# Attention with a beacon prefix, then a gated feed-forward: one key quarter turned earlier, and the last weight third and the output weights issued later

## The chip, the cores and the metric

The kernel runs on one core of a Trainium2 chip. The metric is the device time of one execution in microseconds. Four executions of the kernel before are given, and one more was profiled.

## The reference

Eight batches of eight heads go through causal attention, each with 16 extra "beacon" keys that every query sees. The result is laid out as a matrix of 4608 tokens by 512 features and goes through a feed-forward layer with a gate.

```python
def _attn_ref(q, k, v, beacon_k, beacon_v):        # q, k, v: (8, 8, 576, 64)
    k_all = np.concatenate([beacon_k, k], axis=2)  # 16 + 576 keys
    v_all = np.concatenate([beacon_v, v], axis=2)
    scores = scale * np.matmul(q, k_all.transpose(0, 1, 3, 2))
...
    scores = np.where(causal, -1000000000.0, scores)
...
    return np.matmul(a, v_all)                     # a: softmax of scores

def _moe_ref(x, w_gate, w_val, w_out):             # x: (4608, 512), d_ff 1536
    gate = np.maximum(x @ w_gate, 0.0)
    val = x @ w_val
    return (gate * val @ w_out)
```

## The kernel before

The whole order of work is written out by hand: every engine runs its own instructions in the order in which the program names them, and waits only where a datum or a buffer is missing.

**Attention.** A batch has 592 key rows (16 beacon rows and 576), cut into five key tiles of 128 rows, the last one short. Its queries are cut into chunks of 240, 256 and 80. A unit of work is one group of four heads, one chunk and one key tile: TensorE makes the scores (line 368), ScalarE the exponentials (line 376), and GpSimd clears what lies above the diagonal (the affine selects of line 384). Two units make a step, seven steps a batch. When the units of a chunk are done, TensorE multiplies the exponentials by the values and by ones (line 418), and VectorE divides (lines 430 to 443). So the first product with the values of a batch waits for the values, for the exponentials and for GpSimd's selects.

**Feed-forward.** A tile is 512 tokens. Twelve "up" groups make it (the gate in line 464, the values in line 473, both four matmuls of 512 columns, then lines 467 and 475), and four "down" groups of twelve matmuls each (line 483) use all twelve slices of `wo`. Up group number nf reads columns 128·nf to 128·nf+127 of `wg` and `wv`. The groups fill TensorE between the attention steps: the plan has seven steps for batch 0, four steps without attention (7 to 10, with 0, 3, 3 and 2 groups), seven steps for batch 1 with one group each (11 to 17), two steps without attention with four groups each (18 and 19), and then batches 2 to 7. `s2` is 11, the first step of batch 1; batch 2 begins with step 20 and batch 3 with step 27.

**Queries and keys must lie transposed.** There are three ways. In batch 0 a quarter (256 rows, four heads) is loaded by SyncE (line 281), cast by VectorE or ScalarE (line 285), turned by eight TensorE transposes (line 300) and copied out of PSUM by VectorE or ScalarE (line 301). In batch 1 GpSimd issues loads that cast on the way (line 289), and TensorE turns them in `turn_two`. From batch 2 on SyncE loads rows (line 244), GpSimd casts them (lines 263 and 259), and SyncE issues transposing DMAs (line 268).

**Weights.** The first 256 columns come by SyncE and are cast (lines 339, 345). All others are loaded by GpSimd with a cast on the way: `load_w` issues one DMA for each of two groups (line 330), `load_wo` one DMA for six slices (line 348).

**The queues.** SyncE issues its DMAs in program order, and so does GpSimd; GpSimd's DMA issues stand in one line with its selects and casts. Eight DMAs of a queue have semaphores of their own: in the compiled order the ninth waits until the first has landed. The lists `after(step, ...)` (later half of a step), `between` (after the first unit's scores), `mid` (after the first unit's exponentials) and `behind` fix where an action stands. The values of batch 1 are loaded by SyncE behind a one-element memset on GpSimd (line 241, `held`), which stands on GpSimd's queue behind the eight loads of batch 1's queries and keys.

In step 0 of batch 0 the order is: scores of the first unit, `turn_next`, exponentials of the first unit, `turn_third`, scores of the second unit, `turn_first("q", 1, 0)`. A quarter is named by its half of the rows and its half of the heads: ("k", 0, 1) is keys, first half of the rows, second four heads.

Of the kernel before, what the change touches and what calls it, by code (L numbers as in the profile page):

```python
# [159 lines left out]
def kernel(  # L160
# [38 lines left out]
    wg = const.tile([P, KM, d_ff], BF16, name="wg")  # L199
    wv = const.tile([P, KM, d_ff], BF16, name="wv")  # L200
# [127 lines left out]
    def load_w(dst, src, n0, n1, groups=(0, 1)):  # L328
        for g in groups:
            nc.gpsimd.dma_start(  # L330
                dst[:, 2 * g:2 * g + 2, n0:n1],
                src[2 * g * P:2 * (g + 1) * P, n0:n1].rearrange("(p a) n -> p a n", a=2))
# [14 lines left out]
    def load_wo(i0, i1):  # L347
        nc.gpsimd.dma_start(wo[:, i0:i1],
                            moe_w_out.rearrange("(ko ki) n -> ki ko n", ki=P)[:, i0:i1])
# [177 lines left out]
    with tc.manual_schedule():  # L527
        batches = {}
        dve, act, pool = nc.vector.tensor_copy, nc.scalar.copy, nc.gpsimd.tensor_copy
# [8 lines left out]
        def load_tails(x):  # L538
            x.tails = [x.load_rows(k[x.b, :, 512:]), x.load_rows(q[x.b, :, 512:])]
# [10 lines left out]
        first = batches[0] = Batch(0)  # L550
# [18 lines left out]
        def turn_first(n, i, g, move):  # L569
            ps = f_ps.tile([P, 2, 2, P], BF16, name="f")  # L570
            return first.turn_quarter(n, i, g, ps, move)
# [6 lines left out]
        warm_up(2, 256)  # L578
        first.cast_quarter("k", 0, 1, dve)
        first.cast_quarter("q", 0, 1, act)  # L580

        def turn_two(x, i, k_bank):
            ps = {"k": k_bank.tile([P, NP, 2, P], BF16, name="f" if k_bank is f_ps else "s"),
                  "q": f_ps.tile([P, NP, 2, P], BF16, name="f")}
            for move in [x.turn_quarter(n, i, g, ps[n][:, 2 * g:2 * g + 2],
                                        dve if n == "k" else act)
                         for g in range(2) for n in "kq"]:
                move()
# [12 lines left out]
        def after(step, action):  # L601
            later_half.setdefault(step, []).append(action)

        second = batches[1] = Batch(1)
        s2 = BASE[1]
# [1 line left out]
        held = []  # L607

        def turn_next():
            turn_first("k", 0, 1, dve)()  # L610
            first.cast_quarter("k", 1, 0, dve)
            held.append(turn_first("q", 0, 1, act))
            first.cast_quarter("q", 1, 0, dve)

        def turn_third():
            held.pop()()
            turn_first("k", 1, 0, dve)()

        between[0], mid[0] = turn_next, turn_third
        behind[0] = lambda: turn_first("q", 1, 0, dve)()  # L620
        after(0, lambda: first.cast("v", 0, pool))
# [27 lines left out]
        after(6, lambda: [cast_w(wv, raw_v, 256, g, act) for g in range(2)])  # L649
        second.beacon = second.load_rows(beacon_k[1])  # L650
        load_tails(second)
        for n0 in (768, 1152):
            after(6, lambda n0=n0: load_w(wg, moe_w_gate, n0, n0 + 384))
            after(6, lambda n0=n0: load_w(wv, moe_w_val, n0, n0 + 384))

        def load_second(i):
            for g in range(2):
# [6 lines left out]
            after(7, lambda t=t: second.load("v", t, t == 0))  # L664
        for t in range(NKT):
            after(s2 - 1 + t // 2, lambda t=t: second.cast("v", t, pool))
        after(s2 - 2, lambda: load_wo(0, 6))
        after(s2 - 1, lambda: load_wo(6, 12))

        def cast_small(x):  # L670
            x.beacon = x.cast_rows(x.beacon, dve)
# [186 lines left out]
```

## Time and profile before

| | us |
|---|---|
| median of four executions | 394.16 (392.57 to 394.45) |
| profiled execution: its time | 393.09 |
| profiled execution: its span | 391.4 |

| engine | busy us | share of the span |
|---|---|---|
| TensorE, matmuls (PE) | 375.2 | 96% |
| VectorE (DVE) | 205.4 | 52% |
| ScalarE (ACT) | 192.9 | 49% |
| GpSimd (POOL) | 127.6 | 33% |

The page cuts the span into 40 slices of 9.8 us; a digit is the busy share in tenths. Its chain of work that ended last is 88% TensorE and 6% DMA. The mean granted TensorE clock is 0.991 of full speed. Both DMA queues use the same 16 engines: the queue of SyncE (q1, 139,024 packets, 44.48 MB) and that of GpSimd (q0, 9,056 packets, 5.24 MB as written in bf16). All DMA shares count the time of packets in flight, so a share over 100% means that packets overlap. In a timeline each row has its start, its length, the engine (SPq is SyncE's queue), the line, the operation, what it writes and reads, and in brackets the idle time before it with the instruction that ended it.

### The profile page before, as it was taken

Reading aid. Unit: us, or ns where it says so; the run is one execution under the profiler, and the core shown is the slowest. Engines: PE = TensorE matmul, PEld = TensorE weight load, DVE = VectorE, ACT = ScalarE, POOL = GpSimd, SP = SyncE. Lnnn points to the kernel's source line nnn. Section 1 sums busy time; section 2 is a strip of 40 time slices with the busy share of each in tenths; the row PEclk is TensorE's granted clock in tenths of the full one; section 3 lists DMA queues with packets and bytes.
Section 4 is the critical chain, followed back from the end, with each engine's and each line's share of the span. In section 5 each row is a group of like instructions: output and inputs, shape, how many; then the busy total and the mean of one; then the engine's idle time right before and its main releaser. Section 6 shows DMA issues by size and latency. Waiting matters only on the chain.

```text
span 391.4 us, 10271 instructions
## 1 busy us (share of the span) xinstructions
PE 375.2 (96%) x4297; PEld 188.2 (48%) x4297; DVE 205.4 (52%) x342; ACT 192.9 (49%) x270; POOL 127.6 (33%) x220
## 2 busy tenths in 40 slices
PE   6889859999999999999999999999999999999995
PEld 2554425544555455445454545444545454444443
DVE  4868336653665655476537563666465645512320
ACT  4773436435655655465546554656366633323321
POOL 1697275423553444143514350535020200000000
PEclk9999979999999999999999999999999999999999
DMA  8999999777995997399439943996300011002002
GB/s 215 233 177 185 192 179 222 150 173 171 194 146 162 186 210 123 107 205 177 98 110 190 201 87 105 198 173 120 97 28 2 2 65 46 0 32 77 0 28 86
DMA packets 148132, 50.44 MB, mean 129 GB/s; under 512 B 133616, under 2 KB 143600, under 8 KB 148080
## 3 DMA queue, kind: packets, MB, share of 16 engines
q1 hardware_dynamic: 139024, 44.48, 56.1%
q0 software_dynamic: 9056, 5.24, 9.7%
q8 instruction: 35, 0.57, 0.7%
q14 instruction: 17, 0.14, 0.2%
HBM read 38.34 MB, written 9.44 MB: 122 GB/s over the span
## 4 chain that ended last, share of the span: by engine, by line
PE 88%; DMA 6%; POOL 2%; ACT 2%; issue 1%; SPq 0%; DVE 0%; POOLq 0%
PE f L483 24%; PE f L464 23%; PE s L473 12%; PE f L473 10%; PE s L368 8%; PE ab L418 7%; PE os L418 3%; DMA raw<-in_v_dram 3%; DMA wg<-in_moe_w_gate_dram 2%; ACT e L376 1%; DMA wide<-in_q_dram 1%; PE f L300 1%; PE f L418 1%; POOL wv L330 1%; POOL hwide L289 0%
## 5 line engine op out<-in xcount | busy, mean ns | idle before, releaser
L376 ACT ACTIVATE e<-s 128x1024 bf16<-128x1024 f32 (+2 forms) x112 | 104.8, 963 | 29.0 <-PE s L368 28.9
L464 PE MATMUL f<-xT,wg 128*128 128x512 bf16 x432 | 112.2, 382 | 0.3 <-DMA hwide<-in_k_dram 0.3
L467 ACT ACTIVATE g<-f 128x512 f32<-128x512 f32 x108 | 64.5, 597 | 82.3 <-PE f L464 80.3
L483 PE MATMUL f<-wo,hT 128*128 128x512 bf16 (+1 forms) x444 | 96.7, 374 | 0.0
L384 POOL TENSOR_SCALAR_AFFINE_SELECT e<-e 128x512 bf16<-128x512 bf16 (+2 forms) x80 | 47.0, 599 | 149.9 <-ACT e L376 144.8
L430 DVE RECIPROCAL r<-os 128x80 f32<-128x80 f32 (+2 forms) x43 | 57.6, 1339 | 58.0 <-PE os L418 58.0
L475 DVE TENSOR_TENSOR hT<-g,s 128x512 bf16<-128x512 f32 x60 | 41.2, 687 | 66.3 <-PE s L473 65.2
L473 PEld LDWEIGHTS <-wv 128*128 128x128 bf16 x432 | 42.4, 98 | 52.7 <-issue 3.1
L483 PEld LDWEIGHTS <-hT 128*128 128x128 bf16 x444 | 41.9, 98 | 47.4
L464 PEld LDWEIGHTS <-wg 128*128 128x128 bf16 x432 | 39.6, 98 | 46.8 <-issue 1.3
L473 PE MATMUL s<-xT,wv 128*128 128x512 bf16 x240 | 61.6, 379 | 0.0
L486 ACT COPY ob<-f 128x512 f32<-128x512 f32 (+1 forms) x37 | 21.3, 575 | 73.9 <-PE f L483 71.9
L475 DVE TENSOR_TENSOR hT<-g,f 128x512 bf16<-128x512 f32 x48 | 33.0, 688 | 37.0 <-PE f L473 32.4
L473 PE MATMUL f<-xT,wv 128*128 128x512 bf16 x192 | 50.2, 384 | 0.2 <-ACT qT L301 0.2
L263 POOL CAST half<-raw 128x512 bf16<-128x512 f32 (+2 forms) x60 | 36.8, 625 | 23.0 <-DMA raw<-in_k_dram 8.7
L418 PE MATMUL ab<-e,v 128*32 128x80 bf16 (+4 forms) x1320 | 39.3, 234 | 4.5 <-POOL e L384 4.5
L368 PE MATMUL s<-qT,kT 64*128 64x80 bf16 (+3 forms) x704 | 36.1, 236 | 1.4 <-ACT e L376 0.9
L418 PEld LDWEIGHTS <-v 128*32 128x32 bf16 (+1 forms) x1408 | 26.5, 98 | 14.5 <-issue 7.2
L368 PEld LDWEIGHTS <-kT 64*128 64x128 bf16 x704 | 20.6, 97 | 25.9 <-issue 23.8
L418 PE MATMUL os<-e,ones 128*32 128x240 bf16 (+4 forms) x660 | 32.2, 233 | 0.0
L259 POOL CAST v<-raw 128x512 bf16<-128x512 f32 (+1 forms) x40 | 26.6, 668 | 15.5 <-DMA raw<-in_v_dram 15.0
L443 DVE TENSOR_TENSOR xT<-ab,r 128x480 bf16<-128x480 f32 (+2 forms) x45 | 24.9, 554 | 0.8
(66 smaller groups left out, 136.4 us busy)
## 6 DMA issues: line engine op xcount, KB each, us to landing
out_dram<-ob SPq DMA_DIRECT2D x35, 256.0 KB, 2.2
raw<-in_q_dram SPq DMA_DIRECT2D x25, 256.0 KB, 4.8
raw<-in_v_dram SPq DMA_DIRECT2D x24, 256.0 KB, 5.2
raw<-in_k_dram SPq DMA_DIRECT2D x19, 256.0 KB, 4.5
raw<-in_v_dram SPq DMA_DIRECT2D x8, 224.0 KB, 3.8
wo<-in_moe_w_out_dram POOLq DMA_DIRECT2D x2, 768.0 KB, 9.1
raw<-in_k_dram SPq DMA_DIRECT2D x6, 224.0 KB, 4.4
raw<-in_v_dram SPq DMA_DIRECT2D x8, 160.0 KB, 4.6
```

Of the source, the lines that this page charges most:

```text
L259: copy(self.v[:n, t].rearrange("p (h a d) -> p h a d", a=2, d=C), raw[:n].rearrange("p (h d a) -> p h a d", a=2, d=C))
L263: copy(h[:n], raw[:n])
L368: nc.tensor.matmul(self.s[:, a, c + j * n:c + (j + 1) * n], kT[rows, 2 * g + j, k0:k0 + P], qT[rows, 2 * g + j, q0:q0 + n], start=True, st ...
L376: nc.scalar.activation(e[:, :k * 4 * n].rearrange("p (k a x) -> p a k x", k=k, a=2), self.s[:, :, :k * 2 * n].rearrange("p a (k x) -> p a ...
L384: nc.gpsimd.affine_select(out=cols[:, :, :m], in_=cols[:, :, :m], pattern=[[0, 4], [1, m]], compare_op=ALU.is_ge, fill=0.0, base=base, cha ...
L418: nc.tensor.matmul(o[:, q0 - cq0:q0 - cq0 + n], w, e[:kr, 2 * (hh % 2) + hh // 2], start=(i == 0 and part != 1), stop=(i == self.last), sk ...
L430: nc.vector.reciprocal(self.r[:, :n], self.os[:, :n])
L464: nc.tensor.matmul(g[:, :n], wg[:, ki, nf * P:(nf + 1) * P], x[:, ki], start=(ki == 0), stop=(ki == KM - 1))
L467: nc.scalar.activation(gs[:, :n], g[:, :n], AF.Relu)
L473: nc.tensor.matmul(u[:, :n], wv[:, ki, nf * P:(nf + 1) * P], x[:, ki], start=(ki == 0), stop=(ki == KM - 1))
L475: nc.vector.tensor_mul(self.h[:, nf, c0:c1], gs[:, :n], u[:, :n])
L483: nc.tensor.matmul(o[:, n], self.h[:, nf, ms * P:(ms + 1) * P], wo[:, nf, n], start=(nf == 0), stop=(nf == NF - 1))
```

## The change

Three things are moved; nothing is added or removed.

- The second key quarter ("k", 0, 1) is turned before the first scores of batch 0, not after them. Its VectorE copy moves with it. The cast of the quarter ("q", 1, 0) moves on VectorE from before to behind the copy of ("k", 1, 0).
- The last third of `wg` and `wv` (columns 1152 to 1535, four DMAs) is issued on GpSimd's queue behind the eight loads of batch 1's queries and keys and the memset that holds batch 1's values, not ahead of them.
- The two halves of `wo` are each issued one step later: the first behind the casts of the first two value tiles of batch 1, the second behind those of the next two.

```diff
         first.cast_quarter("q", 0, 1, act)
+        turn_first("k", 0, 1, dve)()
...
         def turn_next():
-            turn_first("k", 0, 1, dve)()
             first.cast_quarter("k", 1, 0, dve)
             held.append(turn_first("q", 0, 1, act))
-            first.cast_quarter("q", 1, 0, dve)

         def turn_third():
             held.pop()()
             turn_first("k", 1, 0, dve)()
+            first.cast_quarter("q", 1, 0, dve)
...
-        for n0 in (768, 1152):
-            after(6, lambda n0=n0: load_w(wg, moe_w_gate, n0, n0 + 384))
-            after(6, lambda n0=n0: load_w(wv, moe_w_val, n0, n0 + 384))
+        after(6, lambda: load_w(wg, moe_w_gate, 768, 1152))
+        after(6, lambda: load_w(wv, moe_w_val, 768, 1152))
...
-        after(s2 - 2, lambda: load_wo(0, 6))
-        after(s2 - 1, lambda: load_wo(6, 12))
+        after(s2 - 2, lambda: load_w(wg, moe_w_gate, 1152, 1536))
+        after(s2 - 2, lambda: load_w(wv, moe_w_val, 1152, 1536))
+        after(s2 - 1, lambda: load_wo(0, 6))
+        after(s2, lambda: load_wo(6, 12))
```

In the compiled order the other differences follow from these: four issues (line 330) stand behind the memset of line 241 on GpSimd, each `wo` issue (line 348) stands one block further back, up group 9 on TensorE waits for the weights' four DMAs, and SyncE's order is the same in both kernels.

## The prediction

> **What bounds the kernel now.** I read the page's slices first, then who waited on TensorE, then the chain, then SyncE's queue. The slices:
>
> ```profile
> PE   6889859999999999999999999999999999999995
> PEclk9999979999999999999999999999999999999999
> DMA  8999999777995997399439943996300011002002
> ```
>
> TensorE is full from slice 6 (58.7 us) on. Its one hole behind the start is slice 5, where the clock drops as well. The DMA engines are full in the same stretch. The waits of TensorE up to 100 us name one long one, and the chain of that stretch tells where it comes from:
>
> ```profile
> PE ab L418 <- POOL e L384: 4.5, 1, 4.5
> ```
>
> ```profile
> 40.44 0.09 POOL raw L241
> ...
> 41.39 10.14 DMA raw<-in_v_dram
> 51.53 0.05 issue
> 51.58 0.62 POOL v L259
> 52.21 0.78 issue
> 52.99 0.60 POOL e L384
> 53.59 0.04 issue
> 53.63 0.59 PE ab L418 x6
> ```
>
> Batch 1's values are held until the memset at 40.44, land at 51.53, and GpSimd casts them, issues half of `wo` (0.78) and clears the exponentials before TensorE resumes at 53.63. TensorE had stopped at 49.11. The table by stages shows what follows:
>
> ```profile
> 53.63:60.50 6.87, 6.87 (x73) 2.98 (x73) 3.00 (x3) 2.48 (x3) 4.19 (x8) 0.56 1.05 168
> ```
>
> The granted clock is 0.56 for 6.87 us. This is what the change is near, and by this view alone it should pay. The view that decides is another one, SyncE's queue in order of time. From 40.55 to 123 us no row of it is more than 0.8 us behind the end of the one before: SyncE issues without a rest, first batch 1's values, then all of batches 2 and 3. The last transposed keys and queries that the first step of each needs are these:
>
> ```profile
> 86.48 1.24 SPq L268 DMA_TRANSPOSE kT<-half  x1
> 87.81 1.21 SPq L268 DMA_TRANSPOSE qT<-half  x1
> ...
> 118.67 1.22 SPq L268 DMA_TRANSPOSE qT<-half  x1
> ```
>
> By the DMA view of 87 to 90 and of 118 to 120 us a query transpose lands 2.4 us after its issue starts: 90.2 and 121.1. TensorE reaches batch 2's first scores at 92.82, so slack there is 2.8 us. At batch 3 it is none:
>
> ```profile
> 120.73 0.81 PE L368 MATMUL s<-qT,kT 64*128 64x240 bf16 x12
> ```
>
> Twelve such score matmuls take 0.60 at 44.68 and at 92.82. Here they take 0.81: the last four stand until about 121.2, when the queries have landed. So behind TensorE's own work lies a second path of almost the same length, SyncE's queue.
>
> **The change, part by part.**
>
> *The key quarter.* Eight transposes (0.64, the row at 10.33) go ahead of the first scores, which move from 7.75 to about 8.2; the first exponentials move from 8.37 to 8.8. The VectorE copy (0.69) starts at 8.25 and not 8.94, the next cast ends 0.7 earlier, the second scores start at 10.45 and not 10.90 (then ScalarE's query copy, behind the first exponentials, is last). But the cast of ("q", 1, 0) now stands behind a key copy: cast 10.95 to 11.45, turn to 12.1, copy to 12.9, against 12.81 before. The scores that waited for this copy (12.86) start at 12.95. Sum: +0.1. Bounds: −0.5 if the second scores' gain were carried on, +0.5 if the first scores' delay were.
>
> *The last weight third.* Four issues of 0.72 (2.86 us of GpSimd) leave the place ahead of batch 1's loads. These eight can be issued from 29.4 on, held by the rule that the ninth waits for the first: the fourth issue after it, 0.8 each, gives a memset at about 36.1 and not 40.44. SyncE's queue starts 4.3 us earlier. What it meets is the engines' work. From 28.6 to 53 us they are full; packets of the two queues show the rates:
>
> ```profile
> q0 software_dynamic: 465, 0.48, 93.1%
> q1 hardware_dynamic: 448, 0.11, 28.9%
> ```
>
> That is 45 to 48 us: 155 `wo` packets a us, and one value packet beside each. Alone, values run at 850 a us (3,398 in the 4 us from 49), batch 1's loads at 704 (3,519 in the 5 us from 38). Now the four weight DMAs lie beside the values: 1,024 packets of 768 bytes, some 200 a us with one value packet each, 39.4 to 44.4. The first two value tiles (2,048 packets) have 900 by then and the rest in 1.4 us; with 1.3 to land, they are there at 47.0, not 51.5. With the 2.1 us of cast, issue and select TensorE resumes at 49.1. It gets there at 48.1, since the stalls of `turn_two` on its loads (0.29 and 0.30) and the wait behind them go, 1.0 in all. So 53.63 becomes 49.1 (−4.5), a gap of 1.0 in place of 4.52, and the half clock is gone: the up group in it took 1.82 + 1.71, the next one at full clock (60.50) 0.97 + 0.86, so 1.7 there, and of the other 3.34, some of it at full clock, 1.2. Together −2.9. Bounds: 0 if values land as before, −8.4 if no gap is left.
>
> Its new deadline: group 9 needs the third at about 50.5 and it has landed by 46: no cost.
>
> *The output weights.* First half issued at about 47.7 and moving from 50, second at 51.5 and moving behind it, 768 packets at 155 a us each: landed at about 61.3. The first down group would read slice 6 at 66.52 − 7.4 + 1.35 = 60.5, so it waits 0.8; bounds 0 and 2.5. Each issue (0.82) lies on GpSimd ahead of selects and casts; the first one was on the path before as well, the second is hidden by the selects' waits for ScalarE. At the first down group TensorE is therefore 6.5 ahead.
>
> *Where this goes.* It does not reach the end, because SyncE's queue is not 6.5 us ahead. The bytes that have to move before batch 2's keys are the same, and the engines were full already. At 60 us, before: `wo` done at 59.4, SyncE's queue alone for 5 us (48.4 to 53.4). After: `wo` done at 60, SyncE's queue alone for 5 us (44.4 to 49.2, less 0.8 without packets). Between 53.4 and 55 the engines were nearly idle (58 GB/s, with 185 after it), so 1.1 us of work is lost before and 0.8 after. Shift of SyncE's queue: −0.3. Bounds: −4.3, its start's own shift, if packets shared the engines for free, and +1. Then batch 2's first step stands: TensorE is there at 93.07 − 6.5 = 86.6 and waits 3.4 for the queries at 90.0. It keeps 3.0. At batch 3 it is there at 118.2 and waits for 120.8: 2.6 more. From there on the order is as before.
>
> A rule speaks against the change here. Trainium skill, *DMA: Bandwidth & Descriptors*, section "Issuing engines are not separate DMA queues": transfers of all issuing engines interleave on the same 16 engines, and another queue saves only issue time. The row above shows one packet beside the other, at no loss for `wo`. Were the sharing free, as that row alone suggests, the sum would be −4.3; by the rule it is −0.3. I take the rule, for the full engines.
>
> Sum against the profiled execution: 393.09 + 0.1 − 0.4 = 392.8. The same step from the median of 394.16 is **393.9**. The 0.4 are SyncE's 0.3 and what is left of the wait at 121.
>
> **The rivals.** "Measurable" is 0.5% here, 2.0 us.
>
> *The queue does come forward.* SyncE starts 4.3 us earlier and keeps it, because value packets slip in beside the weights' unseen. For it: 448 packets slipped in at 45 to 48. Against: from 53 on the queue is short of engine time. Then batch 3's queries land at 116.8, and the time is 394.16 − 4.3 = 389.9. Chance 0.15, with smaller shifts over 2.0 in it.
>
> *Slower: the wait ahead of batch 3 stops the clock.* Before, the gap of 4.5 us was paid early and hidden by the slack up to 121. Now TensorE stands at batch 2 (3.4) and batch 3 (2.6). The row: a gap of 4.52 is followed by 6.87 us at 0.56. Trainium skill, *TensorE: Matmul & The Clock Gate*, Part 1: half rate after an idle window of about 3.4 us, full rate after a busy one, windows free-running. By the row alone 2.6 is far from 4.5 and costs 0; by the rule it is 0.8 short of the least gap that can hold a window. Behind batch 3 no slack is left, so it costs 3.4 in full: 393.9 + 3.4 = 397.3. It decides from a gap of 3.4 at batch 3. At batch 2 the same loss is harmless, as it fills the wait at batch 3. Chance 0.13; with SyncE's queue over 2 us late, 0.17 for slower.
>
> *The change does nothing at 49 us.* The third beside the values keeps them to 51.5. TensorE's gap stays, slack at batch 2 and 3 as before: 394.2. Chance 0.08.
>
> **How the numbers follow.** Forecast 0.60, nothing at 49 us 0.08: same 0.68. Faster 0.15. Slower 0.17. Its own range is 392.5 to 395.5 (queue −1.5 to +1.5). The range is 391.6 to 396.8: it leaves out a tenth at each end, most of the first rival and most of the second.
>
> **What would show it.** TensorE's wait at 53 us and the half clock are gone, values landed at 46 to 48, first down group at 59 to 62. Batch 2's query transpose is still issued at 87 to 88 and batch 3's at 118 to 119. The waits of TensorE name line 368 with a releaser on SyncE's queue or qT, 2 to 4 us each, at about 86 and 118. The hole in slice 5 moves to slices 8 and 12. I am wrong if these transposes come over 2 us earlier, if batch 2's scores start before 89, or if the clock drops at 120.

## The result, and the profile after

| | kernel before | changed kernel |
|---|---|---|
| median | 393.38 us (63 executions, 391.99 to 396.07) | 392.21 us (42 executions, 388.98 to 394.43) |
| profiled execution: its time | 393.09 us | 391.63 us |
| profiled execution: its span | 391.4 us | 389.9 us |

The ratio is 0.9965, with a 95% interval of 0.9954 to 0.9977: about 1.4 us faster (the two medians differ by 1.2), inside the 0.5% that the prediction called no change. The four executions whose median, 394.16, the prediction starts from are among the 63.

The slices of the page of the changed kernel, to be held against the three rows that the prediction shows first:

```profile
PE   7879979998999999999999999999999999999995
PEclk9999989999999999999999999999999999999999
DMA  8999999978995996499449943995300011002002
```

The hole in slice 5 has shrunk (7 where there was 5), and the clock there is 8 and not 7. There is a small new hole in slice 9 (88 to 97 us). TensorE's largest group of waits (their sum, their number, the longest), and the chain from 37.7 to 52 us:

```profile
PE ab L418 <- POOL e L384: 5.2, 4, 2.4
```

```profile
37.72 0.09 POOL raw L241
...
38.67 10.28 DMA raw<-in_v_dram
48.95 0.05 issue
49.00 0.62 POOL v L259
49.62 0.80 issue
50.42 0.60 POOL e L384
51.03 0.04 issue
51.07 0.59 PE ab L418 x8
```

It is the same chain as before, earlier by 2.6 us: the memset that releases the values starts at 37.72 and not 40.44, the values land at 48.95 and not 51.53, TensorE resumes at 51.07 and not 53.63, after a gap of 2.42 us and not 4.52. But that wait now has company: 5.2 us in four waits, where it was one of 4.5. The clock behind it, from the table by stages (start and end, length, then the busy time of each engine; the clock is the third number from the end):

```profile
51.07:54.50 3.43, 3.43 (x33) 1.46 (x33) 2.05 (x2) 1.03 (x2) 3.42 (x7) 0.57 1.11 171
```

Half the clock for 3.43 us, against 6.87 us before. The first down group starts at 62.41 (before 66.45 in the same view) and batch 2's first scores at 88.91 (before 92.82): TensorE is 3.9 us ahead. SyncE's queue is not. These are the issues of the last query transposes that the first steps of batches 2 and 3 need, shown for before at 87.81 and 118.67. Below, "the last query transpose" of a batch always means this one.

```profile
86.73 1.21 SPq L268 DMA_TRANSPOSE qT<-half  x1
88.00 0.57 SPq L244 DMA_DIRECT2D raw<-in_beacon_k_dram  x1
88.62 0.42 SPq L244 DMA_DIRECT2D raw<-in_k_dram  x1
```

```profile
117.39 1.21 SPq L268 DMA_TRANSPOSE qT<-half  x1
```

They are 1.1 and 1.3 us ahead. Where TensorE gives the difference back is seen on GpSimd from 92 us, and on TensorE at 95.77. First the same two casts of the kernel before, with no wait ahead of them, then the changed kernel:

```profile
94.81 1.17 POOL L263 CAST half<-raw 128x512 bf16<-128x512 f32 x2
```

```profile
92.48 0.61 POOL L263 CAST half<-raw 128x512 bf16<-128x512 f32 x1 [1.53 <-DMA raw<-in_k_dram]
93.65 0.62 POOL L263 CAST half<-raw 128x512 bf16<-128x512 f32 x1 [0.55 <-DMA raw<-in_q_dram]
94.49 0.64 POOL L259 CAST v<-raw 128x512 bf16<-128x512 f32 x1 [0.23 <-DMA raw<-in_v_dram]
95.08 1.81 POOL L384 TENSOR_SCALAR_AFFINE_SELECT e<-e 128x512 bf16<-128x512 bf16 x3
```

```profile
95.77 0.29 PE L418 MATMUL ab<-e,v 128*32 128x128 bf16 x8 [1.70 <-POOL e L384]
```

GpSimd's selects for batch 2 stand behind casts of batch 3's first tiles, and those casts wait for loads that SyncE issued at 88.62 and later, right behind batch 2's transposes. TensorE waits 1.70 us. The same happens at 112.21 (0.73). 3.9 − 1.7 − 0.7 leaves 1.5 us, and the two spans differ by 1.5. Batch 3's first scores come at 119.61 (before 120.73, where the last four of them waited about 0.2 more). Behind them the changed kernel is 1.3 us ahead, and it still is at 200.75 (before 202.04).

### The profile page after: what moved, and what is told of

Its sections match the earlier page's. It is cut to its first block, busy times and chain, and to the rows that moved or that the text cites. A ratio compares the mean times of both kernels' runs of the same rounds, so it can differ in the third digit from the quotient of the medians.

```text
span 389.9 us, 10272 instructions
## 1 busy us (share of the span) xinstructions
PE 374.0 (96%) x4297; PEld 187.2 (48%) x4297; DVE 204.4 (52%) x342; ACT 192.9 (49%) x270; POOL 128.2 (33%) x220
## 4 chain that ended last, share of the span: by engine, by line
PE 79%; DMA 10%; SPq 5%; POOL 3%; DVE 1%; issue 1%; ACT 0%; POOLq 0%; DVEq 0%
PE f L483 23%; PE f L464 21%; PE s L473 11%; PE f L473 9%; PE ab L418 6%; PE s L368 6%; DMA raw<-in_v_dram 6%; SPq L244 3%; PE os L418 2%; DMA wv<-in_moe_w_val_dram 2%; DMA raw<-in_k_dram 1%; SPq L281 1%; DMA raw<-in_q_dram 1%; POOL e L384 1%; SPq L268 1%
## 5 line engine op out<-in xcount | busy, mean ns | idle before, releaser
L473 PE MATMUL f<-xT,wv 128*128 128x512 bf16 x192 | 49.4, 379 | 0.4 <-DMA wv<-in_moe_w_val_dram 0.2
```

Of the source, the lines that this page charges most:

```text
L473: nc.tensor.matmul(u[:, :n], wv[:, ki, nf * P:(nf + 1) * P], x[:, ki], start=(ki == 0), stop=(ki == KM - 1))
```

## The experiments

The theory on record, called A below: the change wins some microseconds at TensorE by 89 us, and SyncE's queue, which hardly comes forward, takes most of them back by 121 us. The main rival: TensorE's own work is the bound all along, and the change is worth just what the median shows. Changes of time in microseconds are the ratio's distance from 1, times the median of the executions of the kernel before that were taken together with the run.

### One part alone

The first kernel has only the edit at the start, the second only the weights' (the other lines of the diff undone).

> Only the edit at the start (second key quarter turned ahead of the first scores, the cast of the query quarter behind a key copy); weights as before. Theory on record: +0.1 us on the kernel before (bounds -0.5 and +0.5), and nothing at the end of that, since the wait at 53 us is behind it: ratio 1.000. Rival, that the measured gain of 1.2 us comes from the start (in the changed kernel the second scores stand 1.1 us earlier): -1.2 us, ratio 0.997.

Measured: ratio 0.9991 (0.9973 to 1.001), −0.4 us, which cannot be told from zero.

> Only the last weight third and the output weights move; the start as before. Theory on record: all of the measured gain is here, -1.0 to -1.5 us against before, equal to the changed kernel within 0.3 us; batch 2's first scores at 88.5 to 89.5 us and batch 3's at 119.3 to 120. Rival (start pays): 0 against before, with the scores of batch 3 at 120.7 us.

Measured: ratio 0.9969 (0.9948 to 0.9989), −1.2 us, beside 0.9965 for the whole change. Most of the gain lies in the weights. The profiled execution was 0.4 us over its own median and had batch 2's scores at 90.1 and batch 3's at 120.4, later than expected; a last wait of 0.45 us for a query transpose stands at 121.31. That the start is worth exactly nothing isn't shown, as the interval reaches to −1.1 us.

### A shorter queue by moving stores to ScalarE

```diff
+                if self.m0 < 1024:
+                    nc.scalar.dma_start(out[m:m + P, n], ob[:, n])
+                    continue
                 later_sp.append(
```

> The kernel before, with the output stores of the first two feed-forward tiles issued from ScalarE's queue, so that SyncE's queue is rid of 5 to 8 issues of 0.4 to 0.9 us ahead of batch 3's last query transpose. Theory A (in the kernel before TensorE's own work and SyncE's queue end at batch 3 within 0.4 us of each other, so a shorter queue brings only the rest of the wait at 121): -0.2 to -0.5 us. Theory B (SyncE's queue alone bounds the kernel before): -2 to -3 us.

Measured: ratio 1.0091 (1.0064 to 1.0117), +3.6 us.

> The changed kernel with the same stores moved to ScalarE's queue. Theory A (the changed kernel has won 4 us at TensorE by 89 us and loses most of it to SyncE's queue by 120): batch 3's last query transpose comes 2 to 3 us earlier, and the time falls by 1.5 to 2.7 us against the changed kernel, -2.7 to -4 against before. Rival (TensorE itself is the bound and the change was worth only 1.2 us at 53 us): the same small effect as on the kernel before, -0.2 to -0.5 us. The difference of the two effects tells them apart.

Measured: ratio 1.013 (1.0098 to 1.0162), +5.1 us. Both theories missed, because the edit brings a wait of its own. ScalarE's timeline and TensorE's in the changed kernel with this edit:

```profile
71.32 0.38 ACTq L489 DMA_DIRECT2D out_dram<-ob  x1
71.81 1.56 ACT L376 ACTIVATE e<-s 128x960 bf16<-128x960 f32 x2 [6.44 <-DMA raw<-in_q_dram]
```

```profile
72.83 0.39 PE L368 MATMUL s<-qT,kT 64*128 64x80 bf16 x12 [3.66 <-ACT e L376]
```

ScalarE did no work for 6.44 us. In its order one store (71.32) stood there ahead of the exponentials, and the profile puts the end of the wait down to a load of SyncE's queue. TensorE waited 3.66 us for these exponentials. A second such wait, of 5.21 us, stands at 79.06, and in the kernel before with this edit there are three (5.63, 3.06 and 2.78 us). The stores behind 112 us had none. Why these stores had to wait is not settled. So the two kernels measure these waits, and not a shorter queue. They tell nothing of A.

### A shorter queue by leaving values out

```diff
+            if x == "v" and b in (2, 3):
+                return
             raw = self.raw[x, t] = stage.tile(...)
...
+            if x == "v" and self.b in (2, 3):
+                nc.gpsimd.memset(self.v[:n, t], 0.01)
+                return
             raw = self.raw.pop((x, t))
```

> The kernel before without the loads of the values of batches 2 and 3: GpSimd fills these values with 0.01 in place of the casts, so this part of the computation is left out. It takes some 2.6 MB off SyncE's queue ahead of batch 3's scores, and TensorE's work is unchanged. Theory A (TensorE's own work ends at batch 3 within 0.4 us of the queue): -0.2 to -0.5 us against before. Theory B (queue alone is the bound before): -3 us or more.

Measured: ratio 0.9991 (0.9979 to 1.0004), −0.4 us, and at most −0.8 by the interval.

> The changed kernel, with the values of batches 2 and 3 left out and filled with 0.01 in the same way. Theory A (TensorE's gain of about 4 us at 89 us is kept if the queue isn't in the way): -3.5 to -4.5 us against before, -2.5 to -3.3 against the changed kernel, and the waits of 1.7 and 0.7 us at 96 and 112 us are gone. Rival (the change is worth 1.2 us and no more): the distance to the kernel before without these values is again 1.2 us.

Measured: ratio 0.9894 (0.9862 to 0.9926), −4.2 us against before. This is the pair that decides. The same relief of the queue is worth about 0.4 us in the kernel before and about 2.8 us in the changed one. Without the queue in the way the change is worth 3.8 us; with it, 1.4. (The edit also takes the casts of these values, and so their waits for loads, off GpSimd. It does not part that from the transposes.) TensorE's waits of this kernel (its lines count five more than before's) show which went:

```profile
PE ab L423 <- POOL e L389: 3.3, 2, 3.0
```

What stands here is the wait for batch 1's values, 2.98 us at 51.02; those of 1.70 and 0.73 are gone.

### More loads on the queue

Extra loads of 256 KB, at step 14, between batch 2's (the lines that allocate their tile are left out here):

```diff
                 at(s, lambda u=u: batches[b].load(*u))
+                if b == 2 and j in (9, 10):
+                    at(s, lambda j=j: nc.sync.dma_start(
+                        pools["extra"][:, j - 9]..., v[2, :, :P]...))
```

> The kernel before with two more loads of 256 KB on SyncE's queue among batch 2's loads, into a tile that nobody reads. By the rows of such loads there (1.0 to 1.2 us each) the queue is 2.2 us later from about 68 us on. Theory A (no slack at batch 3): the last query transpose of batch 3 lands at 123.3 and not 121.1, and the time grows by 1.8 to 2.4 us. Rival (TensorE bound, queue with slack): 0.

Measured: ratio 0.9999 (0.9982 to 1.0017), nothing. A's expectation failed. The last query transposes for batch 2 and batch 3 in this kernel:

```profile
89.76 1.21 SPq L268 DMA_TRANSPOSE qT<-half  x1
...
118.82 1.22 SPq L268 DMA_TRANSPOSE qT<-half  x1
```

The first is issued 1.95 us later than before and lands at 92.2, still ahead of TensorE (92.82 before; 93.5 in this execution, which was later from its start on: its clock was half up to 21.5 us). The second is only 0.15 us later. Between the two, three rows of SyncE that had been stretched in the kernel before (2.45, 2.77 and 1.99 us, at 98, 107 and 114) took 1.12, 1.42 and 1.21. So in the kernel before the queue seems to have been waiting there, and could make up nearly 2 us; the trace doesn't name what it waited for. That the queue is without slack at batch 3 was misread.

> The changed kernel with the same two loads. Theory A (the queue bounds the changed kernel from 89 to 120 us): +1.8 to +2.4 us against the changed kernel, so that it is again about 1.2 us faster than the kernel before with these loads. Rival (TensorE bound): 0.

Measured: ratio 0.9997 (0.9983 to 1.0012), 1.3 us over the changed kernel and only 0.1 under the kernel before with these loads, where A expected 1.2. The cost is less than expected and has another reason: no wait behind the casts is left, but one ahead of batch 2's scores, and the table by stages shows the clock behind it:

```profile
92.02 0.30 PE L368 MATMUL s<-qT,kT 64*128 64x128 bf16 x4 [2.12 <-DMA qT<-half]
```

```profile
92.25:95.62 3.37, 3.37 (x12) 1.20 (x9) 0.00 (x0) 1.44 (x2) 0.61 (x1) 0.51 0.98 210
95.62:99.00 3.38, 3.34 (x42) 1.69 (x42) 1.68 (x3) 1.79 (x4) 2.48 (x5) 1.00 0.75 188
```

Two blocks of four matmuls took 1.69 and 1.68 us in the first stretch and 0.86 in the second. The wait of 2.12 and the 1.65 lost to the clock make 3.8, the whole lead of TensorE.

> The kernel before with four more loads of 256 KB among batch 2's loads, not two. With two, the last query transpose of batch 2 landed 2.0 us later (92.2 us, TensorE there at 93.5) and the time didn't move, and 1.9 of the 2.0 us were made up by batch 3. If the slack at batch 2 is 2.8 us, as the prediction has it, four loads bring a landing at 94.3 to 95, a wait of TensorE of 1.0 to 2.0 us there, and +1 to +2 us at the end. Rival (the queue has slack everywhere in the kernel before): 0.

Measured: ratio 1.0084 (1.0057 to 1.011), +3.3 us; the profiled execution's own difference is 2.3. The last query transpose lands at 93.2, 3.0 us later than before, and TensorE is there at 93.1: the 2.8 us of slack at batch 2 are used up, but no wait stands there. TensorE waits in the other place, as it does in the changed kernel:

```profile
99.67 0.29 PE L418 MATMUL ab<-e,v 128*32 128x128 bf16 x8 [1.45 <-POOL e L384]
```

So the kernel before is insensitive to two loads and pays for four. Its 3.3 is above the range that A gave, and the part of it that is not this wait isn't settled.

### Later casts, and another order of the loads

```diff
-        fetch(3, BASE[3] - STEPS - 2, 2)
+        fetch(3, BASE[3] - STEPS - 2, 3)
```

The last number is the count of steps from a load to its cast.

> The changed kernel with GpSimd's casts of batch 3's loads, and the transposes behind them, one step later (three steps behind the loads, not two). Theory A, refined by the trace: TensorE's waits of 1.7 us at 96 and 0.7 us at 112 are selects that stand on GpSimd behind casts whose loads have not landed; one step (4.4 us) later the loads have landed and the waits go. But the last query transpose of batch 3 stands one step later as well, so TensorE waits there instead: -1 to +1 us against the changed kernel. Rival (these waits follow TensorE's own pace): no change in the waits, +1 us or more.

Measured: ratio 1.0056 (1.0031 to 1.0082), +2.2 us against before and 3.6 against the changed kernel. The waits at 96 and 112 us are gone, as expected, and one of 0.94 us for queries at 97.89 is new. The one ahead of batch 3 is larger than allowed for, and the clock drops behind it as well:

```profile
122.09 0.29 PE L368 MATMUL s<-qT,kT 64*128 64x128 bf16 x4 [3.27 <-DMA qT<-half]
```

```profile
122.65:126.06 3.41, 3.08 (x50) 1.47 (x36) 0.66 (x1) 0.93 (x2) 0.00 (x0) 0.50 0.33 71
```

The second kernel keeps the later casts and puts batch 3's values behind the queries and keys of the first step (k0 q0 k1 q1 k2 q2 k3 q3 v0 v1 v2 k4 q4 v3 v4).

> As the run with late casts, and batch 3's loads in another order: all queries and keys that its first step needs, then values 0 to 2, then the last key and query tile and values 3 and 4. So the casts come one step later and the last query transpose of the first step doesn't. Nothing is left out. Theory A: the waits at 96, 112 and 120 us all go, and the 4 us that TensorE is ahead at 89 us reach the end: -2 to -2.8 us against the changed kernel, -3.3 to -4.2 against before, as in the run without values. Rival (the queue's bytes alone set batch 3's start): no more than -1 us against the changed kernel.

Measured: ratio 1.0002 (0.9985 to 1.0019), nothing against before, 1.5 us over the changed kernel. The wait of batch 3 for its queries is not gone either (1.50 us at 122.31). The wait that had been taken away at 96 came back at 112.92, with 1.61 us, and GpSimd's timeline shows why:

```profile
110.54 1.17 POOL L263 CAST half<-raw 128x512 bf16<-128x512 f32 x2 [5.99 <-issue]
```

With queries and keys first, this is the seventh cast into the six `half` buffers, and it starts 0.1 us after the first key transpose had landed (110.4) and set one free. That the buffers are the cause is read from this; it wasn't tried with more of them.

### The stores held back on SyncE's queue

`run_sp` issues the stores that have come due.

```diff
-            pools["osb"] = main.enter_context(tc.tile_pool(name="osb", bufs=6))
+            pools["osb"] = main.enter_context(tc.tile_pool(name="osb", bufs=9))
...
-            run_sp()
+            if not s2 < s <= BASE[3]:
+                run_sp()
```

> The changed kernel with the output stores of the first two feed-forward tiles still on SyncE's queue, but held back until step 28, behind batch 3's transposes and batch 4's first loads (nine buffers for them in place of six, nothing left out). By the rows of the changed kernel this takes six issues of 0.4 to 0.9 us, with the gaps about 3 us, out of SyncE's queue between 78 and 119 us, 1.8 of them ahead of batch 2's last query transpose. Theory A: that transpose lands 1.5 to 2 us earlier, batch 3's loads start as much earlier, TensorE's waits at 96 and 112 us fall from 2.4 to under 1 us, and the time is 1 to 2.5 us under the changed kernel, -2.2 to -3.7 against before. Rival (what is left of the change's gain is limited by the engines' bytes or by TensorE, not by the order on the queue): within 0.5 us of the changed kernel.

Measured: ratio 0.9905 (0.9878 to 0.9931), 389.44 us: 3.7 us under before and about 2.4 under the changed kernel. The changed kernel without values has a median of 389.41. Nothing is left out here. The last query transpose for batch 2 lands at 86.9 (89.1 in the changed kernel), GpSimd's casts at 91 us no longer wait, and the last query transpose for batch 3 is issued 3.7 us earlier than in the changed kernel:

```profile
91.36 1.17 POOL L263 CAST half<-raw 128x512 bf16<-128x512 f32 x2
92.47 0.64 POOL L259 CAST v<-raw 128x512 bf16<-128x512 f32 x1
93.06 1.22 POOL L384 TENSOR_SCALAR_AFFINE_SELECT e<-e 128x512 bf16<-128x512 bf16 x2
```

```profile
113.70 1.22 SPq L268 DMA_TRANSPOSE qT<-half  x1
```

```profile
117.27 0.60 PE L368 MATMUL s<-qT,kT 64*128 64x240 bf16 x12
```

That transpose lands at 116.1, and TensorE comes at 117.27: now the queue is ahead. Later casts still wait for loads (up to 1.45 us, at 104.73), but behind 52 us TensorE has no wait over 0.25 us up to batch 3. Of the versions run here that compute everything this is the fastest. The kernel before with its stores held back was not run. That the 2.4 us need the change as well is argued from the kernel before without values, which gained 0.4.

## Why the prediction was right, and where it was wrong

The forecast was no change (393.9 from 394.16, −0.3), with a local gain given back to SyncE's queue. The mechanism is shown by the pair without values and by the held stores. The gain was larger than forecast by about 1 us. The range held although TensorE's lead at batch 2 was 3.9 us and not the 6.5 of the sum: by the prediction's own mechanism the end follows SyncE's queue, so this error hardly reaches the total. The steps were these.

**Values at 47.0, gap of 1.0.** Right in direction, too early. The memset came at 37.72 and not 36.1: the eight loads ahead of it started at 29.92 and stood 1.6 us in four waits, of which the profile puts three down to VectorE. The second value tile landed at 48.95. So the step at 53.63 gained 2.6 us and not 4.5.

**The half clock is gone.** Wrong: it lasts 3.43 us in place of 6.87, which saves 1.5 us (6.87 × 0.44 less 3.43 × 0.43) and not 2.9. Even this belongs to these two executions. The table at the end has gaps of 4.26 and 4.33 us with one such stretch, in kernels that are the kernel before up to there, and one of 2.32 with two, in a kernel that is the changed one up to there.

**`wo` waits 0.8.** 0.1 by the row: the first down group took 2.90 us and 2.76 before. The lead there is 4.0 (2.6 and about 1.5) and not 6.5. No wait stands at the groups that read the last third.

**SyncE's queue shifts by −0.3.** The size that missed: −1.1 at batch 2 and −1.3 at batch 3, inside the −1.5 to +1.5 on which the forecast's own range rests. Its start came forward by 2.7 us, and by 62 us that was lost. Three issues in a row of the changed kernel, then the third of them before:

```profile
54.69 3.71 SPq L244 DMA_DIRECT2D raw<-in_k_dram  x1
58.50 4.28 SPq L244 DMA_DIRECT2D raw<-in_q_dram  x1
62.87 1.29 SPq L244 DMA_DIRECT2D raw<-in_v_dram  x1
```

```profile
62.00 1.19 SPq L244 DMA_DIRECT2D raw<-in_v_dram  x1
```

The two long issues lie where one or both halves of `wo` were under way (issued at 49.58 and 53.50, landed 8.7 and 10.3 us later). This fits the argument on the full engines, and no run tests it. The first key transpose for batch 2 then took 1.44 us in place of 3.33 and ended at 73.75, 0.7 us ahead of 74.47. Neither of the two sums came out, −0.3 by the shared engines and −4.3 by free sharing; the measured shift is nearer to the first. This term is the difference between forecast and result.

**Waits of 3.4 and 2.6 at line 368.** Wrong place. At batch 2 TensorE came 2.3 us later than worked out, and met the queries as they landed. It waited at line 418 instead, for selects behind casts that waited for loads of the same queue. The sum is the same kind of loss (2.4 us), but I had followed only the transposes, and not the casts that stand on GpSimd ahead of work for TensorE.

**"At batch 3 it is none."** Wrong for the queue of the kernel before, as the two extra loads show: it can make up nearly 2 us between batch 2 and batch 3. The slack of 2.8 at batch 2 stands: 2.0 us later was free, 3.0 was not, though TensorE then waited behind the casts and not for the queries.

**The start, +0.1.** The second scores came at 9.84 (forecast 10.45, before 10.90) and the next ones at 12.46 (12.95 forecast, 12.86 before). By 22.2 us the 0.4 us were nearly gone again (22.24, before 22.32), behind a wait of 0.9 for exponentials.

**What would show it.** Of the three signs of being wrong one came, by a hair: batch 2's scores started at 88.91, before 89. The transposes came 1.1 and 1.3 us earlier and not over 2, and the clock from 113 to 122 us is 1.00. Of the other signs several failed: the values landed at 48.95 and not by 48, the first down group started at 62.41 and not by 62, the transposes were issued at 86.73 and 117.39, each just ahead of the stretch named, the half clock was shorter and not gone, and no wait names line 368 behind the queue.

**The rivals.** The queue's start did not carry through (1.1 of the 2.7 us by which it came forward, where 4.3 were forecast). TensorE's gap at 49 us did shrink, so the change did what it says. The clock rival was not met in the changed kernel, whose waits behind 52 us are 1.70 us at most. But what it feared does happen, and at shorter waits than I wrote. *TensorE: Matmul & The Clock Gate*, Part 1, of the Trainium skill speaks of an idle window of about 3.4 us, and from it I took a gap of 3.4 as the point that decides. A wait of 2.12 us was followed by half the clock in the changed kernel with two extra loads, and one of 3.27 us in that with later casts. The measurement decides: 3.4 us is not the least gap. No single length is, as waits of 2.15 and 2.20 us were followed by full clock.

## What to carry to other kernels

When an early wait is taken away, ask which second path ends at nearly the same time, and follow it through every engine that waits for it: here SyncE's queue reached TensorE by transposes and also by GpSimd's casts, which stand ahead of its selects. An edit whose gain is given back may become worth its full size together with a second one: with eight stores held back that nobody waits for, the two together were worth 3.7 us where the change alone was worth 1.4. A transfer should not be moved to an engine whose own work is on the path, unless it can be issued there without waiting.

## What the runs showed of the hardware

- **The clock and short waits.** Each row names waits of TensorE behind 26 us, and how long the granted clock stood at 0.50 next to each. These stretches come in two lengths only, and cost half of their length in TensorE's work.

| kernel | wait, us | ends at, us | half clock, us |
|---|---|---|---|
| before; start alone; stores on ScalarE; four extra loads | 4.52; 4.41; 4.23; 4.53 | 53.63; 54.20; 54.20; 54.23 | 6.8 each |
| before without values; before with two extra loads | 4.33; 4.26 | 54.26; 55.48 | 3.4 each |
| changed, stores on ScalarE | 3.66 | 72.83 | 3.4 |
| changed, later casts | 3.27 | 122.09 | 3.4 |
| weights alone; changed without values; changed with two extra loads | 3.15; 2.98; 2.71 | 51.22; 51.02; 50.91 | 3.4 each |
| changed; later casts; held stores | 2.42; 2.43; 2.27 | 51.07; 50.37; 50.64 | 3.4 each |
| changed, later casts and other order | 2.32 | 50.55 | 6.8 |
| changed, stores on ScalarE | 2.15; 2.20 | 50.58; 80.68 | none |
| changed, two extra loads | 2.12 | 92.02 | 3.4 |
| before, stores on ScalarE; changed | 1.77; 1.70 | 89.15; 95.77 | none |

  So the length of the wait alone does not decide between none, one and two of these stretches, and no run here shows what else does. In the start, where TensorE has many short waits, a stretch (22.0 to 25.5 us, before with four extra loads) stood behind waits of only 0.85 and 0.90 us.
- **A store on another engine's queue.** ScalarE stood without work for 6.44 us around a store whose own issue took 0.38, until, by the profile, a load issued by SyncE had landed. Stores issued there between 112 and 122 us, at 0.35 each, stood 0.4 to 0.5.
